# Attention with pooled keys, then a two-layer MLP: second-layer products split into 256-column halves, and other hand-over times in the planner

## The chip, the cores and the metric

The kernel runs on one core of one Trainium2 chip. The metric is the device time of one execution in microseconds; the time given for a kernel is the median of its runs. A core has five engines that run side by side, each through its own list of instructions in order: TensorE (PE in the profile; its weight loads are shown as PEld), ScalarE (ACT), VectorE (DVE), GpSimd (POOL) and SyncE (SP, which here only issues transfers). They wait for one another by semaphores.

## What is computed

```python
# q (4, 12288, 128), kv (4, 384, 32, 128), w_sr (128, 128)
kv_pool = kv.reshape(B, H // 4, 4, W // 4, 4, C).mean(axis=(2, 4))
k = v = kv_pool.reshape(B, -1, C) @ w_sr          # 768 keys per batch
s = (q @ k.transpose(0, 2, 1)) / np.sqrt(C)
a = np.exp(s - s.max(-1, keepdims=True)); a /= a.sum(-1, keepdims=True) + 1e-9
x = (a @ v).reshape(49152, 128)
h = x @ w_in                                      # w_in (128, 2048)
out = (h * (1.0 / (1.0 + np.exp(-1.702 * h)))) @ w_out   # w_out (2048, 128)
```

The arrays are float32; the kernel multiplies in bfloat16 with float32 accumulation.

## The kernel before

**Tiles.** The 49152 rows are cut into 96 groups of `G` = 512. Attention has 6 chunks of 128 keys per group, the MLP 16 chunks (`FCH`) of 128 hidden columns per group. Both run the same two-step pattern. A *fill* is a first-layer product of 512 columns into one bank of PSUM: keys by queries (line 350) or `w_in` by `x` (line 596). ScalarE then applies Exp (line 352) or the gelu (line 598) to `K` = 3 such banks at once, 1536 columns wide, and writes bfloat16 to the large SBUF tile `ag`, which has 34 frames of three chunks. A *drain* reads a chunk back from `ag` as the operand of a second product that accumulates in another bank: `drain_attn` for tiles of 128 queries, three tiles to a bank (line 363, 129 columns, the last being the row sum), and `drain_moe` for one chunk of a group (line 606, 512 columns, weights `w_out_sb[:, fc, :]`). After 16 drains of the MLP, VectorE transposes the bank to `o_sb` (line 617) and SyncE stores it in four transfers. Drains of the very last group have a form of their own, `drain_last`, with products of 128 columns on line 634.

**Banks.** Of the eight banks of PSUM, 0 to 2 and 3 to 5 take the fills alternately, so fill `p` writes the banks that the activation of fill `p - 2` must have read. Banks 6 and 7 (in the start-up, when fills are one or two chunks wide, also 2 and 5) hold the accumulations and the smaller helpers: pooling of the keys, projections, transposes.

**Order.** `R` = 2 rounds: attention of 48 groups, then their MLP, then the same for the other 48. The list `seq` holds the fills with their widths, the list `todo` the drains. Some activations are computed on VectorE instead of ScalarE, by `early_fill` (lines 403 to 477, fills on lines 409 and 415).

**The planner.** Nothing is scheduled by the compiler: the program is recorded in the order that the loop at line 797 chooses, and each engine runs it in that order. The loop keeps a reckoned time `now` on TensorE, in units of one 512-column product. `end[p]` is the reckoned end of activation `p`. After fill `n + 2` it emits drains and helpers until the next would end after

```python
limit = end[-1] - len(seq[n + 3][1]) - HANDOVER
```

that is, so late that the next fill could not be done when the activation before it ends. It then emits the next fill. A drain may begin no sooner than `end[needs] + HANDOVER`; a fill no sooner than `end[p - 2] + HANDOVER / 2`; an activation `HANDOVER / 2` after its fill. With few free frames in `ag` (`room`) the limit is set aside. `free` holds when a bank is reckoned to be empty, `dve` when VectorE is.

Of the kernel before, what the change touches and what calls it, by code (L numbers as in the profile page):

```python
# [24 lines left out]
def kernel(  # L25
    ctx, tc, q, kv, w_sr, moe_w_in, moe_w_out, out,
):
    nc = tc.nc
# [7 lines left out]
    FCH = d_ff // 128  # L36
    scale = 1.0 / (C ** 0.5)
    G = 512
    SG = 4 * G
    NG = B * N // G  # L40
# [3 lines left out]
    K = 3  # L44
    T = 128
    TS = 3
# [38 lines left out]
    def acc(key=None):  # L85

        nonlocal last_acc
        last_acc = next_acc()
        turns.append(last_acc)
        turns.remove(last_acc)  # L90
        if key:
            closes[last_acc] = key
        return banks[:, last_acc, :]
# [7 lines left out]
    def close(key, then):  # L101
        for m in [m for m in closes if closes[m] == key]:
            del closes[m]
            free[m] = then


    now = 0.0
# [165 lines left out]
    for m in range(0, 128, 32):  # L273
        p = slice(m, m + 32)
# [23 lines left out]
    w_out_sb = cpool.tile([128, FCH, C], BF)  # L298
# [28 lines left out]
    def room_ahead():  # L327
        return K * len(free_frames())
# [6 lines left out]
    def weights(c):  # L335
        if c[0] == "a" and c[1] in early:
            return ag[:, (c[1] - early[0]) * JC + c[2], :]
        if c[0] == "a" and c[1:] in rolling:
            return aside[:, rolling.index(c[1:]) % K, :]
        if c[0] == "m" and c[1:] in lent:  # L340
            return aside[:, (len(rolling) + lent.index(c[1:])) % K, :]
        return ag[:, slot_of[c], :]
# [249 lines left out]
    o_of = {}  # L592
# [4 lines left out]
                             x[:, g % (4 * XS) * G:(g % (4 * XS) + 1) * G], start=True, stop=True)  # L597
        nc.scalar.activation(place([("m",) + c for c in chunks]), ps, AF.Gelu_apprx_sigmoid)  # L598

    def drain_moe(g, fc):  # L600
        if g == NG - 1:
            drain_last(g, fc)
            return
        if fc == 0:
            o_of[g] = acc(("o", g))
        nc.tensor.matmul(o_of[g], w_out_sb[:, fc, :], weights(("m", g, fc)),  # L606
                         start=(fc == 0), stop=(fc == FCH - 1))
        if (g, fc) in lent:
            used.append((g, fc))
        else:  # L610
            del slot_of["m", g, fc]
        if fc == FCH - 1:
            close(("o", g), max(now, dve - 1.0) + EVACUATE)
            on_dve(3.6)

            o_sb = opool.tile([128, 512], F32, name="o_sb")
            nc.vector.transpose(o_sb, o_of.pop(g))  # L617
            for m in range(4):
                nc.sync.dma_start(out=out_r[g, m],
                                  in_=o_sb[32 * m:32 * m + 32, :].rearrange("i (b j) -> i b j", j=32))  # L620
# [34 lines left out]
    seq, todo = [], []  # L655
    todo_early = [("a", t, a) for t in range(NT) for a in range(2) if (t // TS * TS + TS - 1) // 4 in early]
    for n in range(R):
        part = [c for c in chunks if c[0] // (NG // R) == n]
        while part:
            m = sizes.pop(0) if sizes else K  # L660
            seq.append(("a", part[:m]))
            part = part[m:]
        begin = n * NT // R
        if n == 0:
            begin = SPLIT * TS
# [7 lines left out]
        while flat:  # L673
            m = K if len(flat) > sum(rest) else rest.pop(0)
# [36 lines left out]
    def prepare(p):  # L711

        nonlocal now
        kind, part = seq[p]
        for i, jc in part:
            if (kind, i) not in begun:
                begun.add((kind, i))
                (background if kind == "a" else background_moe)(i)
            while kind == "a" and ((key_and_value, i // GB, jc) in extras or (transpose_q, i) in extras):
                f, *args = extras.pop(0)  # L720
                now = max(now, free[next_acc()]) + COST[f][0]
                f(*args)
                free[last_acc] = copied(f)
# [19 lines left out]

    FIXED, CHUNK, SWITCH, HANDOVER, EVACUATE = 0.295, 1.978, 6.0, 1.0, 4.5
    COST = {pool_chunk: (1.9, 2.6), key_chunk: (0.3, 2.4), value_chunk: (0.3, 2.4),
            transpose_q: (1.05, 4.2), early_fill: (1.0, 5.5), key_and_value: (0.55, 3.5),
            transpose_pooled: (0.9, 3.6), make_k: (0.8, 3.2), make_v: (0.8, 3.7)}
# [1 line left out]
    SMALL = 0.26  # L751
    RECIPROCAL = 8.2
    PAUSE = 4.0
    end, extra_at = [], 0.0
    source, dve = None, 0.0
    early_left = 2 * (G // T) * EARLY

    def on_dve(cost):
        nonlocal dve
        dve = max(dve, now + 1.0) + cost  # L760
# [8 lines left out]
    def fill(p):  # L769
        nonlocal now  # L770
        if p >= len(seq):
            return
        kind, part = seq[p]
        prepare(p)
        if p == 4:
            turns.insert(0, 2)
        if p == narrow - 5:
            for m in (2, 5):
                turns.remove(m)
        if p == narrow:  # L780
            assert not any(m in closes for m in (2, 5))
            now = max(now, free.pop(2), free.pop(5))
        lo = K * (p % 2)
        (fill_attn if kind == "a" else fill_moe)(part, banks[:, lo:lo + len(part), :])
        if p >= 2:
            now = max(now, end[p - 2] + HANDOVER / 2)
        now += len(part)
        begin = max(now + HANDOVER / 2, end[p - 1] if p else 0.0)
        if p and kind != seq[p - 1][0]:
            begin += SWITCH  # L790
        end.append(begin + FIXED + CHUNK * len(part))
# [4 lines left out]
    jobs(2)  # L796
    for n in range(len(seq)):
        fill(n + 2)
        jobs(n + 3)
        while True:  # L800
            room = room_ahead()
            limit = end[-1] - len(seq[n + 3][1]) - HANDOVER if n + 3 < len(seq) else 1e9
            bank = free[next_acc()]
            f = None
            if extras and now >= max(extra_at, bank):
                f, *args = extras[0]
            if steps and dve <= now + 2.0:
                early_step()
            near = todo and todo[0][0] == "m" and todo[0][2] > 10
            if not f and not near and not steps and early_todo and early_fits(min(n + 2, len(seq) - 1), *early_todo[0]) and dve <= now + 2.0 and now >= bank:  # L810
                f, args = early_fill, early_todo[0]
            if f and max(now, bank) + COST[f][0] > limit + (0.0 if f is early_fill else 4.5) and room >= 4 * K:
                f = None
            if f:
                now = max(now, bank) + COST[f][0]
                f(*args)
                free[last_acc] = dve + 1.0 if f is early_fill else copied(f)
                if f in (transpose_pooled, make_k, make_v):
                    on_dve(2.5)
                extra_at = max(now + PAUSE, dve + 1.5 if f in (transpose_pooled, make_k, make_v) else 0.0)  # L820
                if f is early_fill:
                    pass
                else:
                    extras.pop(0)
                continue
            if not source:

                if todo_early and not any(early_waits(t) for t in range(todo_early[0][1], todo_early[0][1] + TS)):
                    source = todo_early
                else:  # L830
                    source = todo
            if not source:
                break
            kind, i, c = source[0]
            needs = at[("at" if kind == "a" else kind, i, c)]
            cost = K * SMALL if kind == "a" else 1.0
            halved = kind == "a" and i // TS < SPLIT
            first_of = (c == 0 or halved) and (kind == "m" or i % TS == 0)
            if source is not todo_early and (needs > n or (kind == "a" and first_of and at["at", i + TS - 1, c if halved else 1] > n)
                                             or (kind == "m" and first_of and (i, FCH - 1) in lent  # L840
                                                 and made.get((i, FCH - 1), 1e9) > now + 1.0)
                                             or (kind == "a" and (early_waits(i) or first_of and early_waits(i + TS - 1)))):
                if first_of:
                    source = None
                break
            start = now if source is todo_early else max(now, end[needs] + HANDOVER)
            if first_of:
                start = max(start, bank)
            if start + cost > limit and not (room < 2 * K + 1 or (room < 4 * K and start == now)):
                if first_of:  # L850
                    source = None
                break
            now = start + cost
            (drain_attn if kind == "a" else drain_moe)(i, c)
            source.pop(0)
            if kind == "a" and i // 4 in early:
                early_left -= 1
                if not early_left:
                    low = 0
            if (halved or c == (1 if kind == "a" else FCH - 1)) and (kind == "m" or i % TS == TS - 1):  # L860
                source = None
# [31 lines left out]
```

## Time and profile before

| what | value |
|---|---|
| time, median of 3 runs | 948.76 us (948.5 to 948.81) |
| span of the profiled execution | 946.7 us |
| granted TensorE clock | 1.000 |
| ScalarE, gelu on line 598 | 509 instructions, 681.1 us busy, 1489 ns each |
| ScalarE, Exp on line 352 | 192 instructions, 245.6 us busy |
| TensorE, fills on line 596 | 1476 recorded, 379 ns each |
| TensorE, drains on line 606 | 1477 + 17 recorded, 379 ns each |
| weight loads of line 606 | 1520, 98 ns each |
| VectorE, transposes on line 617 | 95 of 717 ns |

A busy time is the union of the records on an engine. A record of a matmul runs from its start to its modelled end, so records of successive matmuls overlap, and so do those of successive activations; what an engine can do per unit of time is read from one start to the next. Some matmul records are missing in a trace, so a gap of one whole product between two records is no idle time; weight loads are counted more fully. The profile has the idle time before an instruction in brackets, with the engine and line whose end ended it.

### The profile page before, as it was taken

What the parts mean: (1) busy time and instruction counts of PE and PEld (TensorE: products, weight loads), DVE (VectorE), ACT (ScalarE), POOL (GpSimd) and SP (SyncE); (2) the same over time, 40 slices, a digit from 0 to 9 for tenths busy, and PEclk for the clock granted to TensorE, in tenths of its full rate; (3) what the DMA queues carried; (4) which work ended last, traced back from release to release, by engine and by line L of the source; (5) the groups of instructions that cost most, each with busy time, mean ns of one, the idle gap of its engine ahead of it and who ended that gap; (6) DMA issues with size and microseconds to landing.
All of it is one profiled execution on the core that took longest, in us unless ns stands there. A gap on an engine that the chain in (4) does not pass through costs nothing.

```text
span 946.7 us, 15374 instructions
## 1 busy us (share of the span) xinstructions
PE 933.9 (99%) x6200; PEld 502.5 (53%) x6314; DVE 575.1 (61%) x1091; ACT 933.5 (99%) x709; POOL 66.5 (7%) x115
## 2 busy tenths in 40 slices
PE   8999999999999999999999999999999999999998
PEld 4677776444444444444446777744444444444444
DVE  5753653011678776667765765376767766777651
ACT  6999999999999999999999999999999999999998
POOL 3101001330000232000000000000000000000000
PEclk9999999999999999999999999999999999999999
DMA  9997943999867799865335683552222222222222
GB/s 210 195 207 168 181 92 52 130 163 170 164 117 114 119 147 119 127 99 87 56 58 105 138 170 84 119 123 42 36 39 40 38 41 34 44 34 45 34 45 46
DMA packets 372856, 95.46 MB, mean 101 GB/s; under 512 B 346720, under 2 KB 370400, under 8 KB 372320
## 3 DMA queue, kind: packets, MB, share of 16 engines
q1 hardware_dynamic: 344000, 62.36, 36.9%
q0 software_dynamic: 28512, 31.99, 22.3%
q8 instruction: 49, 0.80, 0.3%
q14 instruction: 23, 0.19, 0.1%
q10 hardware_dynamic: 272, 0.13, 0.0%
HBM read 52.49 MB, written 48.76 MB: 107 GB/s over the span
## 4 chain that ended last, share of the span: by engine, by line
PE 97%; ACT 1%; DMA 1%; issue 1%; DVE 0%; POOL 0%; POOLq 0%
PE banks L606 35%; PE banks L596 34%; PE banks L363 14%; PE banks L350 12%; ACT ag L352 1%; PE banks L415 1%; DMA x<-in_kv_dram 1%; PE banks L139 0%; PE banks L409 0%; PE banks L634 0%; PE banks L236 0%; POOL x L222 0%; PE banks L161 0%; PE banks L294 0%; PE banks L192 0%
## 5 line engine op out<-in xcount | busy, mean ns | idle before, releaser
L598 ACT ACTIVATE ag<-banks 128x1536 bf16<-128x1536 f32 (+1 forms) x509 | 681.1, 1489 | 0.0
L596 PE MATMUL banks<-x,w_in_sb 128*128 128x512 bf16 x1476 | 405.8, 379 | 1.7
L606 PE MATMUL banks<-ag,w_out_sb 128*128 128x512 bf16 x1477 | 402.6, 379 | 1.7
L352 ACT ACTIVATE ag<-banks 128x1536 bf16<-128x1536 f32 (+2 forms) x192 | 245.6, 1421 | 3.5 <-PE banks L236 2.3
L606 PEld LDWEIGHTS <-w_out_sb 128*128 128x128 bf16 x1520 | 148.3, 98 | 177.2 <-issue 0.2
L596 PEld LDWEIGHTS <-w_in_sb 128*128 128x128 bf16 x1519 | 147.1, 98 | 171.3 <-issue 0.7
L617 DVE STREAM_TRANSPOSE o_sb<-banks 128x512 f32<-128x512 f32 x95 | 68.1, 717 | 171.4 <-PE banks L606 166.9
L363 PEld LDWEIGHTS <-ag 128*128 128x128 bf16 x2268 | 145.5, 98 | 44.6 <-issue 0.3
L363 PE MATMUL banks<-v,ag 128*128 128x129 bf16 x2268 | 163.0, 220 | 0.2
L350 PE MATMUL banks<-qT,kT 128*128 128x512 bf16 x498 | 145.0, 379 | 3.5 <-ACT ag L352 0.5
L442 DVE SCALAR_TENSOR_TENSOR ea<-ea,eb 128x512 f32<-128x512 f32 x132 | 90.4, 685 | 3.7 <-DVE ea L442 0.7
L386 DVE RECIPROCAL rec<-banks 128x3 f32<-128x3 f32 x124 | 22.3, 180 | 85.3 <-PE banks L363 84.9
L389 DVE TENSOR_TENSOR x<-banks,rec 128x384 bf16<-128x384 f32 x124 | 69.1, 557 | 4.3
L350 PEld LDWEIGHTS <-kT 128*128 128x128 bf16 x543 | 45.8, 98 | 25.9 <-issue 2.0
L473 DVE RECIPROCAL eb<-ea 128x256 f32<-128x256 f32 x34 | 57.6, 1724 | 0.5
L466 DVE SCALAR_TENSOR_TENSOR ea<-ea,eb 128x512 f32<-128x512 f32 x68 | 46.5, 683 | 1.9
L173 POOL DMA_DIRECT2D kvs<-in_kv_dram x32 | 40.4, 1323 | 19.3 <-DMA kvs<-in_kv_dram 17.1
L431 DVE TENSOR_SCALAR ea<-banks 128x512 f32<-128x512 f32 x33 | 22.8, 692 | 29.6 <-PE banks L415 29.2
L521 POOL MEMSET gate_tile<- 1x1 f32 x38 | 3.4, 89 | 325.8 <-DVE gate_tile L520 325.8
L453 DVE TENSOR_SCALAR qT<-banks 128x512 f32<-128x512 f32 x17 | 11.8, 692 | 20.7 <-PE banks L409 20.6
L437 DVE SCALAR_TENSOR_TENSOR eb<-eb,ea 128x512 f32<-128x512 f32 x33 | 22.8, 691 | 0.9
L444 DVE SCALAR_TENSOR_TENSOR ag<-ea,ee 128x512 bf16<-128x512 f32 x24 | 16.6, 691 | 1.2
(83 smaller groups left out, 286.3 us busy)
## 6 DMA issues: line engine op xcount, KB each, us to landing
out_dram<-o_sb SPq DMA_DIRECT2D x380, 64.0 KB, 2.0
kvs<-in_kv_dram POOLq DMA_DIRECT2D x32, 384.0 KB, 6.3
q_bf<-in_q_dram POOLq DMA_DIRECT2D x21, 512.0 KB, 6.6
x_bf<-x SPq DMA_DIRECT2D x13, 768.0 KB, 5.6
x<-in_kv_dram POOLq DMA_DIRECT2D x11, 512.0 KB, 10.4
x_bf<-x SPq DMA_DIRECT2D x6, 384.0 KB, 4.6
x<-in_q_dram POOLq DMA_DIRECT2D x5, 256.0 KB, 15.3
x<-in_kv_dram SPq DMA_DIRECT2D x1, 1024.0 KB, 5.0
```

Source lines behind the costliest of these rows:

```text
L173: nc.gpsimd.dma_start(out=kv_sums[b][:, i2], in_=kv_p[b, i, w, :, i2], **({"accum_op": ADD} if n else {}))
L350: nc.tensor.matmul(ps[:, k, :], kTs[i // GB][:, jc * 128:(jc + 1) * 128], rhs, start=True, stop=True)
L352: nc.scalar.activation(place([("a",) + c for c in chunks]), ps, AF.Exp, scale=scale)
L363: nc.tensor.matmul(av_of[u][:, k * (C + 1):(k + 1) * (C + 1)], weights(("a", i, jc))[:, o:o + T], vs[i // GB][:, jc, 0:C + 1], start=(jc = ...
L389: nc.vector.tensor_tensor(to, ps[:, :, 0:C], rec.unsqueeze(2).broadcast_to([128, TS, C]), MUL)
L442: nc.vector.scalar_tensor_tensor(a, a, COEFFS[k], b, ADD, MUL)
L466: nc.vector.scalar_tensor_tensor(a, a, COEFFS[k], b, ADD, MUL)
L473: nc.vector.reciprocal(b[:, m:m + 256], a[:, m:m + 256])
L596: nc.tensor.matmul(ps[:, k, :], w_in_sb[:, fc * 128:(fc + 1) * 128], x[:, g % (4 * XS) * G:(g % (4 * XS) + 1) * G], start=True, stop=True)
L598: nc.scalar.activation(place([("m",) + c for c in chunks]), ps, AF.Gelu_apprx_sigmoid)
L606: nc.tensor.matmul(o_of[g], w_out_sb[:, fc, :], weights(("m", g, fc)), start=(fc == 0), stop=(fc == FCH - 1))
L617: nc.vector.transpose(o_sb, o_of.pop(g))
```

## The change

Three things change. `drain_moe` takes a range of columns, so that a product can be emitted as two of 256 columns, each with its own weight load. The planner's one `HANDOVER` becomes `RELEASE` (from the reckoned end of an activation to whoever waits for it, by kind of activation) and `LATENCY` (from the end of a fill to its activation), and the fixed part of an activation, `FIXED`, goes from 0.295 to 0.25. And where a whole product of the MLP (not a group's first, and not of the last group) would end past `limit` but a half would not, the loop emits the left half, goes on to the next fill, and emits the right half when it gets to the drains again.

```diff
-    def drain_moe(g, fc):
+    def drain_moe(g, fc, lo=0, hi=G):
...
-        nc.tensor.matmul(o_of[g], w_out_sb[:, fc, :], weights(("m", g, fc)),
-                         start=(fc == 0), stop=(fc == FCH - 1))
+        nc.tensor.matmul(o_of[g][:, lo:hi], w_out_sb[:, fc, :], weights(("m", g, fc))[:, lo:hi],
+                         start=(fc == 0), stop=(fc == FCH - 1 and hi == G))
+        if hi < G:
+            return
...
-    FIXED, CHUNK, SWITCH, HANDOVER, EVACUATE = 0.295, 1.978, 6.0, 1.0, 4.5
+    FIXED, CHUNK, SWITCH, EVACUATE = 0.25, 1.978, 6.0, 4.5
+    RELEASE, LATENCY, HALF = {"a": 0.8, "m": 1.6}, 0.95, 0.506
...
-            now = max(now, end[p - 2] + HANDOVER / 2)
+            now = max(now, end[p - 2] + RELEASE[seq[p - 2][0]])
         now += len(part)
-        begin = max(now + HANDOVER / 2, end[p - 1] if p else 0.0)
+        begin = max(now + LATENCY, end[p - 1] if p else 0.0)
...
-            limit = end[-1] - len(seq[n + 3][1]) - HANDOVER if n + 3 < len(seq) else 1e9
+            limit = end[-1] - len(seq[n + 3][1]) - LATENCY if n + 3 < len(seq) else 1e9
...
-            cost = K * SMALL if kind == "a" else 1.0
+            cost = K * SMALL if kind == "a" else HALF if begun_half else 1.0
...
-            start = now if source is todo_early else max(now, end[needs] + HANDOVER)
+            start = now if source is todo_early else max(now, end[needs] + RELEASE[seq[needs][0]])
...
+            if kind == "m" and c and not begun_half and i < NG - 1 and start + cost > limit >= start + HALF:
+                drain_moe(i, c, 0, G // 2)
+                now = start + HALF
+                begun_half = True
+                continue
...
             now = start + cost
-            (drain_attn if kind == "a" else drain_moe)(i, c)
+            if begun_half:
+                drain_moe(i, c, G // 2, G)
+                begun_half = False
+            else:
+                (drain_attn if kind == "a" else drain_moe)(i, c)
```

The built program has 6553 matmuls instead of 6314: 478 of 256 columns take the place of 239 on line 606. All other instructions are the same ones, in another order on TensorE and VectorE.

More of the change, by code (lines that the diff above doesn't have):

```diff
@@ L603, in drain_moe @@
             return
-        if fc == 0:
+        if fc == 0 and lo == 0:
             o_of[g] = acc(("o", g))
-        nc.tensor.matmul(o_of[g], w_out_sb[:, fc, :], weights(("m", g, fc)),
-                         start=(fc == 0), stop=(fc == FCH - 1))
+        nc.tensor.matmul(o_of[g][:, lo:hi], w_out_sb[:, fc, :], weights(("m", g, fc))[:, lo:hi],
+                         start=(fc == 0), stop=(fc == FCH - 1 and hi == G))
+        if hi < G:
+            return
         if (g, fc) in lent:
@@ L754 @@
     end, extra_at = [], 0.0
-    source, dve = None, 0.0
+    source, dve, begun_half = None, 0.0, False
     early_left = 2 * (G // T) * EARLY
@@ L835 @@
             needs = at[("at" if kind == "a" else kind, i, c)]
-            cost = K * SMALL if kind == "a" else 1.0
+            cost = K * SMALL if kind == "a" else HALF if begun_half else 1.0
             halved = kind == "a" and i // TS < SPLIT
-            first_of = (c == 0 or halved) and (kind == "m" or i % TS == 0)
+            first_of = (c == 0 or halved) and (i % TS == 0 if kind == "a" else not begun_half)
             if source is not todo_early and (needs > n or (kind == "a" and first_of and at["at", i + TS - 1, c if halved else 1] > n)
```

## The prediction

> **What bounds the kernel now.** I read the page's first two parts, then the costliest groups, then the timeline at single matmuls, at the start and at the end.
>
> ```profile
> PE 933.9 (99%) x6200; PEld 502.5 (53%) x6314; DVE 575.1 (61%) x1091; ACT 933.5 (99%) x709; POOL 66.5 (7%) x115
> ...
> PE   8999999999999999999999999999999999999998
> ...
> ACT  6999999999999999999999999999999999999998
> ```
>
> TensorE and ScalarE are both at 99%, so occupancy doesn't say which of them sets the time. A TensorE record also holds the matmul's pipeline (379 ns for 512 columns), so I went to the spacing of the starts.
>
> ```profile
> 298.52 14.98 ACT L598 ACTIVATE ag<-banks 128x1536 bf16<-128x1536 f32 x11
> ...
> 301.72 0.81 PE L596 MATMUL banks<-x,w_in_sb 128*128 128x512 bf16 x3
> ...
> 302.37 0.81 PE L606 MATMUL banks<-ag,w_out_sb 128*128 128x512 bf16 x3
> ...
> 303.02 0.81 PE L596 MATMUL banks<-x,w_in_sb 128*128 128x512 bf16 x3
> ```
>
> Each line gives start, length, engine and group. Three matmuls take 0.81 us, so their starts are (0.81 - 0.379) / 2 = 0.215 us apart, and the next three start 0.65 us later, three such steps: no slot is free. Over the whole trace the mean spacing is 215.8 ns behind 512 columns (L596, L606) and 56.7 ns behind 129 (L363). Taking each pair of starts and subtracting the row's spacing (a gap of a whole slot is a missing record), TensorE's gaps come to 0.6 us from 60 us to the end. Before 45 us they come to about 9 us. ScalarE's eleven activations start (14.98 - 1.49) / 10 = 1.349 us apart on average, while the commonest spacing of two 1536-wide ones in the trace is 1.331 us. ScalarE therefore waits a little in nearly every step, and TensorE never does: after 60 us **TensorE's own work sets the time**.
>
> ```profile
> 26.27 0.39 PE L236 MATMUL banks<-ident,x 128*128 128x128 bf16 x4
> 26.97 0.59 PE L350 MATMUL banks<-qT,kT 128*128 128x512 bf16 x2 [0.31 <-ACT ag L352]
> ...
> 940.35 0.59 PE L596 MATMUL banks<-x,w_in_sb 128*128 128x512 bf16 x2
> ...
> 940.78 2.62 PE L634 MATMUL banks<-w_out_sb,ag 128*128 128x128 bf16 x44
> 942.82 0.91 DVE L642 COPY o_sb<-banks 128x128 f32<-128x128 f32 x3 [3.57 <-PE banks L634]
> ```
>
> In the start-up TensorE does wait, for ScalarE here. At the end the last first-layer product starts at 940.35 and only 2.4 us of second-layer work stand behind it: both engines finish together, and copies and stores follow in any order of the work.
>
> **The change part by part.** The built orders of the two kernels have the same activations in the same order, and the same matmuls except that 239 of the 1520 second-layer products on L606 are two of 256 columns.
>
> *The halves, added work.* Two rows give the price of a matmul's beginning: (215.8 - 56.7) / (512 - 129) = 0.4156 ns per column, so 56.7 - 129 x 0.4156 = 3.0 ns remain at zero columns. 239 more beginnings x 3.0 ns = **0.7 us**, on the engine that has no gap. Each half also loads its weights again: 239 x 98 ns = 23.4 us more on PEld, which has 947 - 502 us free. The cover is the matmul that runs meanwhile.
>
> ```profile
> L363 PEld LDWEIGHTS <-ag 128*128 128x128 bf16 x2268 | 145.5, 98 | 44.6 <-issue 0.3
> L363 PE MATMUL banks<-v,ag 128*128 128x129 bf16 x2268 | 163.0, 220 | 0.2
> ```
>
> Here a load of 98 ns stands before each matmul of 129 columns, and they still start 56.7 ns apart with 0.2 us of idle time in 2268: a 256-column half (0.4156 x 256 + 3.0 = 109 ns) covers it better. Without the cover it would be those 23.4 us. The Trainium skill ("TensorE: Matmul & The Clock Gate", section "The mechanism") speaks against the change: weight loads overlap running matmuls only when their row groups differ. All loads here fill 128 rows, so by that rule the sum would be 23.4 us higher; this trace contradicts it, and I take the row.
>
> *The order, moved work.* The new reckoning puts first-layer matmuls (L350, L596) sooner. For each I summed, in both built orders, the durations of all matmuls ahead of it. The difference grows steadily to 8.0 us at the last one: that much second-layer and attention work is left behind it, and where 2.4 us follow the last first-layer product now, about 11 us will. TensorE does not shorten its work by this; it only does the same work later. The price is zero as long as ScalarE can follow, for a first-layer group refills the banks that ScalarE must first have read. So I set "us by which TensorE reaches the group sooner" against "us that ScalarE has waited so far" (starts of two activations less 1.331 us, table loads taken off), both counted from 45 us:
>
> | up to, us | sooner | ScalarE's waits | left |
> |---|---|---|---|
> | 145 | 0.8 | 1.6 | 0.8 |
> | 245 | 1.8 | 2.7 | 0.9 |
> | 345 | 2.3 | 3.5 | 1.2 |
> | 495 | 3.5 | 5.1 | 1.6 |
> | 545 | 4.4 | 5.5 | 1.1 |
> | 645 | 5.2 | 6.7 | 1.5 |
> | 745 | 5.8 | 7.7 | 1.9 |
> | 845 | 6.6 | 8.7 | 2.1 |
> | 920 | 7.4 | 9.4 | 2.0 |
>
> The right column never falls below zero: the advance is nearly the whole of ScalarE's waiting and not more. Both engines are then full at once, and the cover is thin. The deepest fall of the right column at any step is 0.66 us (in the second attention stretch, around 500 to 545 us); where ScalarE cannot be ahead, TensorE waits that long at the bank. Bounds: 0 (fills now are 0.2 us early, which swallows most falls) and 0.66 us; I take **0.3 us**.
>
> *The start-up.* The first moved matmuls come at about 21 us: groups of three L363 matmuls (3 x 56.7 ns = 0.17 us) go from before a first-layer pair to behind it, in about ten places up to 50 us, and at the table's first row the two orders are level again. TensorE's real gaps from 20 to 45 us sum to 1.8 us. If the moves fill all of them the gain is 1.8; if six of ten each open a wait of their own 0.17 us the loss is 1.0. Some moves go one way and some the other, so I take **0**.
>
> *The end.* ScalarE ends some 7 us earlier, TensorE drains alone, and the last product of L634 is again followed by the same copy and store: 946.7 - 942.8 = 3.9 us as now. DVE must empty a bank (L617, 0.72 us) in the time of 16 products, 16 x 215.8 ns = 3.5 us, and two banks alternate, so this hides. Stores (64 KB, four per group, 2.0 us to landing) hide likewise.
>
> *Sum.* On the profiled execution: 946.7 + 0.7 + 0.3 + 0 = 947.7. The median of the runs, 948.76, is 2.1 us above that span, and this does not change: **949.8 us**.
>
> **The rivals.**
>
> *ScalarE sets the time, so its waits are worth their length (faster).* The Trainium skill ("Perfetto Trace Analysis", section "Identifying the Most-Contended Engine") judges TensorE's headroom by MFU and by the weight loads' busy share, and ScalarE's by occupancy. By the 53% of PEld against ScalarE's 99%, ScalarE would be the bound, and the advance of 8.0 us would be gained: 941.5 by that reading. Against it stands the spacing in this trace: 0.6 us of gaps in 880 us. What TensorE can still gain lies before 45 us: 948.76 - 1.8 + 0.7 = 947.7, which is not yet faster by 0.2%. Chance of more: 4%.
>
> *ScalarE cannot give up its waits (slower).* Place: the hand-over from the last first-layer matmul to ScalarE, in every step. Its quickest in the trace is 0.415 us from that matmul's start to the activation's, which the new plan uses almost in full (0.95 of a 0.2158 us slot, plus the slot itself: 0.421 us). Activations that start 1.348 us apart, 17 ns late, are common now even where their matmuls ended in time. If that lateness stays, the advance of up to 7.4 us turns into TensorE's waiting: at most 948.76 + 0.7 + 7.4 = 956.9; if a third stays, 948.76 + 0.7 + 2.5 = 952.0. It decides once more than the spare 2.0 us of the table's last row (its right column) is kept: from there on each microsecond kept is one lost. For it: the margin is thin. Against it: a late ScalarE gets its matmuls earlier, and there the lateness is rarer (with 0.54 to 0.62 us from matmul to activation nearly all spacings are 1.331 us). 26%, mostly near its lower end.
>
> *The halves' loads are not covered (slower).* 948.76 + 23.4 + 0.7 = 972.9. The L363 rows exclude it for equal tiles; 1%, counted in the 26%.
>
> *The change does nothing that can be measured.* That is the forecast itself, with the work merely put off: 70%.
>
> **How the numbers follow.** A measurement of this kernel can tell about 0.2% from no change, which is 1.9 us: 946.9 to 950.7. The likeliest case has 949.8, and its bounds are 948.76 - 1.8 + 0.7 = 947.7 and 948.76 + 0.7 + 0.66 + 1.0 = 951.1, of which the last 0.4 us already lie past 950.7; I count that among the slower ones. The range reaches from 947.7 to the third-kept case, 952.0. Faster 0.04, same 0.70, slower 0.26.
>
> **What would show it.** Right: the record counts on L606 rise by about 239; TensorE's starts after 60 us keep their spacing, with the gaps' sum under 1.5 us; the commonest spacing of activations is 1.331 us and the last 1024-wide one starts near 934 instead of 941 us; between it and the first copy on L642 (old numbering) lies a run of second-layer matmuls alone. Wrong: waits of first-layer matmuls (L350, L596) for ScalarE in the steady stretches, by more than a microsecond in all, or a total below 946.9 us, which would mean that TensorE's slots were not the bound.

## The result and the profile after

The changed kernel takes 956.56 us (median of 4 runs, 956.53 to 956.6), the kernel before 948.78 us in the same comparison: slower by 7.8 us, ratio 1.0083 with an interval of 1.0069 to 1.0097. The forecast was 949.8 us with a range from 947.7 to 952.0, so it was wrong. The profiled execution has a span of 954.8 us.

The page's parts on the engines, the 40 slices and the chain that ended last, of the changed kernel:

```profile
PE 946.4 (99%) x6553; PEld 525.9 (55%) x6553; DVE 572.3 (60%) x1091; ACT 932.4 (98%) x709; POOL 66.7 (7%) x115
...
PE   8999999999999999999999999999999999999998
...
ACT  6999999999999999999999999999999999999994
...
PE 84%; ACT 13%; DMA 1%; DVE 0%; issue 0%; SPq 0%; POOL 0%; DVEq 0%; POOLq 0%
```

Busy shares hardly differ from before. Two things do: ScalarE's last slice is 4 instead of 8, so it stops earlier than TensorE now, and 13% of the chain that ended last has moved from TensorE to ScalarE (1% before). The halves are where they were announced: 474 of them in the row below and 4 in a smaller row, each 272 ns long, 107 ns shorter than a whole product for 256 columns less (groups by shape of the changed kernel; the columns behind the first bar are busy us and mean ns of one, the last is idle time):

```profile
L606 PE MATMUL banks<-ag,w_out_sb 128*128 128x512 bf16 x1266 | 354.4, 379 | 0.0
...
L606 PE MATMUL banks<-ag,w_out_sb 128*128 128x256 bf16 x474 | 129.2, 272 | 0.0
```

The steady stretch of the changed kernel in the timeline (start, length, engine, group):

```profile
703.13 0.81 PE L606 MATMUL banks<-ag,w_out_sb 128*128 128x512 bf16 x3
703.77 0.81 PE L596 MATMUL banks<-x,w_in_sb 128*128 128x512 bf16 x3
704.42 0.81 PE L606 MATMUL banks<-ag,w_out_sb 128*128 128x512 bf16 x3
705.09 0.81 PE L596 MATMUL banks<-x,w_in_sb 128*128 128x512 bf16 x3
705.74 0.38 PE L409 MATMUL banks<-x,w_in_sb 128*128 128x512 bf16 x1
```

Three products take 0.65 us from start to start. The last step but one takes 0.67: TensorE stood still for 24 ns before the fill at 705.09, and that fill started 51 ns after the end of the activation whose banks it refills. After 60 us, 191 fills of lines 350 and 596 have such a gap of over 8 ns, most of 15 to 55 ns, 7.3 us in all (no matmul is missing from this trace), and 190 of them start 50 to 52 ns after the end of an activation. The view of waits shows the longer ones, under the engine of the weight loads; before, and then after (us in all, times, longest):

```profile
PEld L596 <- issue: 0.7, 3, 0.2
```

```profile
PEld L596 <- issue: 7.7, 45, 0.3
```

From its first to its last matmul, TensorE's time less the sum of all its matmuls (at 0.4156 ns per column and 3.05 ns each) is 11.1 us before and 18.0 us after: 6.9 us more standing still. The 239 additional matmuls make 0.7 us more, and the end after the start of the last matmul 0.4 us (946.68 - 943.18 = 3.50 before, 954.75 - 950.82 = 3.93 after). That is the 8.1 us between the two spans, but for rounding.

The end, in the timeline of the changed kernel:

```profile
939.93 7.07 PE L606 MATMUL banks<-ag,w_out_sb 128*128 128x512 bf16 x32
...
946.84 0.67 PE L636 MATMUL banks<-w_out_sb,ag 128*128 128x128 bf16 x9
947.04 0.72 DVE L619 STREAM_TRANSPOSE o_sb<-banks 128x512 f32<-128x512 f32 x1 [2.74 <-DMA out_dram<-o_sb]
947.81 3.23 PE L636 MATMUL banks<-w_out_sb,ag 128*128 128x128 bf16 x55 [0.31 <-DVE o_sb L619]
```

Some 11 us of second-layer work lie behind the last fill, as the built order says, against 2.5 us before. ScalarE's last activations, before and then after:

```profile
934.50 7.57 ACT L598 ACTIVATE ag<-banks 128x1024 bf16<-128x1024 f32 x8
```

```profile
937.82 2.92 ACT L598 ACTIVATE ag<-banks 128x1024 bf16<-128x1024 f32 x3
```

The last of them starts at 939.6 us now, and not near 934: it was 941.0 before. TensorE put 8 us of work off, and ScalarE came only 1.4 us sooner for it.

### The profile page after: what moved, and what is told of

It is laid out like the page before. It is cut to its first block, busy times and chain, and to the rows that moved or that the text cites. A ratio compares the mean times of both kernels' runs of the same rounds, so it can differ in the third digit from the quotient of the medians.

```text
span 954.8 us, 15982 instructions
## 1 busy us (share of the span) xinstructions
PE 946.4 (99%) x6553; PEld 525.9 (55%) x6553; DVE 572.3 (60%) x1091; ACT 932.4 (98%) x709; POOL 66.7 (7%) x115
## 4 chain that ended last, share of the span: by engine, by line
PE 84%; ACT 13%; DMA 1%; DVE 0%; issue 0%; SPq 0%; POOL 0%; DVEq 0%; POOLq 0%
PE banks L596 35%; PE banks L606 33%; ACT ag L352 13%; PE banks L363 8%; PE banks L350 6%; DMA x<-in_kv_dram 1%; PE banks L415 1%; PE banks L409 0%; DMA out_dram<-o_sb 0%; PE banks L636 0%; DVE o_sb L619 0%; PE banks L139 0%; SPq L621 0%; POOL x L222 0%; DVE kT L163 0%
## 5 line engine op out<-in xcount | busy, mean ns | idle before, releaser
L596 PE MATMUL banks<-x,w_in_sb 128*128 128x512 bf16 x1519 | 410.4, 378 | 0.0
L606 PE MATMUL banks<-ag,w_out_sb 128*128 128x512 bf16 (+1 forms) x1740 | 408.2, 350 | 0.0
L606 PEld LDWEIGHTS <-w_out_sb 128*128 128x128 bf16 x1759 | 171.4, 98 | 180.9 <-issue 1.0
L350 PE MATMUL banks<-qT,kT 128*128 128x512 bf16 x543 | 148.4, 378 | 1.8 <-DVE kT L163 0.4
```

Source lines behind the costliest of these rows:

```text
L350: nc.tensor.matmul(ps[:, k, :], kTs[i // GB][:, jc * 128:(jc + 1) * 128], rhs, start=True, stop=True)
L596: nc.tensor.matmul(ps[:, k, :], w_in_sb[:, fc * 128:(fc + 1) * 128], x[:, g % (4 * XS) * G:(g % (4 * XS) + 1) * G], start=True, stop=True)
L606: nc.tensor.matmul(o_of[g][:, lo:hi], w_out_sb[:, fc, :], weights(("m", g, fc))[:, lo:hi], start=(fc == 0), stop=(fc == FCH - 1 and hi == G))
```

## What ScalarE's records say

The prediction took the commonest distance of two starts, 1.331 us, for ScalarE's own pace. Successive 1536-wide activations near 702 us, read from the records one by one (start in ns, length, to the next start, to the next end):

```text
before: 701904 1470 1331 1343      after: 701974 1727 1354 1342
        703235 1482 1331 1344             703328 1715 1347 1344
        704566 1495 1387 1344             704675 1712 1331 1342
        705953 1452 1347 1342             706006 1723 1336 1345
        707300 1447 1331 1344             707342 1732 1347 1342
```

The starts jump; the **ends** are 1.342 to 1.345 us apart, in both kernels. The same instruction is 1.45 to 1.74 us long in these records, and longer in the kernel whose fills come earlier, as the groups by shape show, before and after:

```profile
L598 ACT ACTIVATE ag<-banks 128x1536 bf16<-128x1536 f32 x501 | 673.6, 1496 | 0.0
```

```profile
L598 ACT ACTIVATE ag<-banks 128x1536 bf16<-128x1536 f32 x501 | 673.2, 1697 | 0.0
```

Same busy time, 0.2 us longer records: they start earlier and end no sooner. That an engine's pace is read from one start to the next, as the table of the profile before was explained, therefore doesn't hold for ScalarE here. By the ends, ScalarE's waits in the 654 wide steps after 45 us come to 1.0 us before (mean distance 1.3449 us, against 1.3433 in the changed kernel) and to nothing after. Counted as the prediction did, by the starts less 1.331 us, the same steps give 9.1 us.

The Trainium skill ("Perfetto Trace Analysis", section "DVE / Act Engine Instruction (TENSOR_ADD, Activation, etc)") puts the reported start where the instruction begins to execute and the reported end where its writes are acknowledged. The end agrees with these runs in so far as a waiting fill starts 50 to 52 ns behind it. A start that moves by 0.25 us while the ends keep their pace doesn't fit a start of execution.

So theory A was formed: `FIXED` + 3 x `CHUNK` is the planner's idea of an activation. With 0.295 it is 6.229 slots x 215.8 ns = 1.3442 us, just above the measured 1.3433 to 1.3435; with 0.25 it is 6.184 slots = 1.3345 us, 9 ns below it. In some 690 steps the plan runs 6.2 us ahead of what ScalarE can do, and TensorE stands at the banks.

## The experiments

The times of the first four are beside 948.49 us of the kernel before, those of the last three beside 948.38 us.

**One constant back,** in the changed kernel:

```diff
-    FIXED, CHUNK, SWITCH, EVACUATE = 0.25, 1.978, 6.0, 4.5
+    FIXED, CHUNK, SWITCH, EVACUATE = 0.295, 1.978, 6.0, 4.5
```

> The changed kernel with FIXED back at 0.295, all else as changed (224 products halved). Theory A (FIXED = 0.25 reckons an activation at 6.184 slots of 215.8 ns = 1.3345 us, while in both traces the ends of two activations lie 1.3435 us apart; 9 ns short in each of some 690 steps sends TensorE 6 to 8 us ahead, and it waits for ScalarE): with 0.295 the plan has 1.3442 us, the fills are no longer drawn ahead (0.4 us at the last, against 7.8), TensorE's gaps after 60 us fall from 6.6 to under 1.5 us, and the time is before plus the halves, 948.8 + 0.7 = 949.5, at most 951. Theory B (RELEASE and LATENCY, the narrower window, make the waits): as slow as the change, 955 to 957. Theory C (the halves cost more than 3 ns each): 955 to 957 too, with normal spacing before first-layer matmuls but longer ones at the halves.

Measured: 949.81 us, ratio 1.0013 (1.0004 to 1.0023). Theory A holds: TensorE's gaps at fills fall from 7.3 to 0.5 us, with the halves and the new hand-over times in place. Waits, and the wide activations, of this kernel:

```profile
PEld L596 <- issue: 1.0, 6, 0.2
```

```profile
L598 ACT ACTIVATE ag<-banks 128x1536 bf16<-128x1536 f32 x501 | 673.7, 1494 | 0.0
```

The records are short again: ScalarE is no longer handed its work early.

**The constant alone,** in the kernel before:

```diff
-    FIXED, CHUNK, SWITCH, HANDOVER, EVACUATE = 0.295, 1.978, 6.0, 1.0, 4.5
+    FIXED, CHUNK, SWITCH, HANDOVER, EVACUATE = 0.25, 1.978, 6.0, 1.0, 4.5
```

> The kernel before with FIXED = 0.25 alone: no halves, one HANDOVER. In its built order the last fill is drawn 8.0 us ahead, as in the changed kernel (7.8). Theory A: TensorE waits at fills for some 6 to 7 us, 955 to 957 us, last activation no more than 2 us sooner than before. Theories B and C: 948.8, as before.

Measured: 955.79 us, ratio 1.0076 (1.0061 to 1.0091). Without a half and without a new hand-over time it loses nearly all that the change loses. Its waits:

```profile
PEld L596 <- issue: 9.9, 56, 0.4
```

**The halves alone:** the changed kernel, with its `drain_moe` and the new branch of the loop, but with every constant and every use of `HANDOVER` as before (against the changed kernel; the other two uses are left out here):

```diff
-    FIXED, CHUNK, SWITCH, EVACUATE = 0.25, 1.978, 6.0, 4.5
-    RELEASE, LATENCY, HALF = {"a": 0.8, "m": 1.6}, 0.95, 0.506
+    FIXED, CHUNK, SWITCH, HANDOVER, EVACUATE = 0.295, 1.978, 6.0, 1.0, 4.5
+    HALF = 0.506
...
-            limit = end[-1] - len(seq[n + 3][1]) - LATENCY if n + 3 < len(seq) else 1e9
+            limit = end[-1] - len(seq[n + 3][1]) - HANDOVER if n + 3 < len(seq) else 1e9
...
-            start = now if source is todo_early else max(now, end[needs] + RELEASE[seq[needs][0]])
+            start = now if source is todo_early else max(now, end[needs] + HANDOVER)
```

> The kernel before with the halves alone (238 products halved, FIXED 0.295, HANDOVER as before). Theory A: 948.8 + 238 x 3.0 ns = 949.5, within 0.5. Theory B: the same. Theory C: 955 to 957.

Measured: 949.30 us, ratio 1.0008 (0.9999 to 1.0018). The 238 halved products cost about 0.8 us (between nothing and 1.7 us by the interval), which fits the 3 ns each that were reckoned, and bring nothing. The rule of the Trainium skill that the prediction weighed, that weight loads overlap running matmuls only when their row groups differ ("TensorE: Matmul & The Clock Gate", section "The mechanism"), would have made them cost 238 x 98 ns = 23 us; the measurement decides against it here.

**ScalarE by itself.** In the kernel before:

```diff
-        nc.tensor.matmul(o_of[g], w_out_sb[:, fc, :], weights(("m", g, fc)),
-                         start=(fc == 0), stop=(fc == FCH - 1))
+        if fc not in (3, 7, 11):
+            nc.tensor.matmul(o_of[g], w_out_sb[:, fc, :], weights(("m", g, fc)),
+                             start=(fc == 0), stop=(fc == FCH - 1))
```

> The kernel before with the second-layer products of chunks 3, 7 and 11 left out of each sum (of all groups but the last): 61.5 us less work on TensorE, ScalarE's work unchanged. It measures ScalarE by itself. Theory A (ScalarE was full already; its floor is 1.3435 us from end to end, and the 1.331 us between starts is only how early it is handed its next instruction): ends stay 1.343 us apart, records of activations are long (about 1.7 us), and the time is no more than 2 us below before: 946.5 to 949. Rival (the floor is 1.331 us, and the 9.4 us above it were waits for TensorE): ends 1.331 us apart and 938 to 941 us.

Measured: 948.09 us, ratio 0.9996 (0.9986 to 1.0005). With 61.5 us less to do, TensorE gives back 0.4 us, too little to tell from nothing. Its waits and the wide activations:

```profile
PEld L596 <- issue: 113.2, 444, 0.6
```

```profile
L598 ACT ACTIVATE ag<-banks 128x1536 bf16<-128x1536 f32 x501 | 673.2, 1698 | 0.0
```

TensorE now waits in nearly every step of the MLP, the fill again 51 ns after the activation's end, and ScalarE's ends stay 1.343 us apart (185 of 186 distances from 200 to 450 us are 1.342 to 1.344). This is the pace that nothing but ScalarE sets. The rival's 938 to 941 us falls, and with it the prediction's figure of 1.331 us.

**The change without its halves:**

```diff
-            if kind == "m" and c and not begun_half and i < NG - 1 and start + cost > limit >= start + HALF:
+            if False and kind == "m" and c and not begun_half and i < NG - 1 and start + cost > limit >= start + HALF:
```

> The changed kernel without its halves (FIXED 0.25, RELEASE and LATENCY as changed, every second-layer product whole). The window in which a fill may be emitted is 6.184 - 1.6 - 3 - 0.95 = 0.63 slots, less than one product, so the planner often leaves the rest of a step empty and puts the products off: the last fill is drawn 16.2 us ahead in the built order. Theory A (what the plan draws ahead comes back as TensorE's waiting, less about 1.5 us): 962 to 965 us; the halves then repair a loss that the narrow window itself makes. Rival (the new window is harmless and FIXED alone costs): 955 to 956, as with FIXED = 0.25 alone.

Measured: 968.05 us, ratio 1.0207 (1.019 to 1.0224), worse than both theories had it, and well beyond the rival. The timeline of this kernel shows the empty piece of each step:

```profile
704.09 0.81 PE L596 MATMUL banks<-x,w_in_sb 128*128 128x512 bf16 x3
704.74 0.81 PE L606 MATMUL banks<-ag,w_out_sb 128*128 128x512 bf16 x3
705.44 0.81 PE L596 MATMUL banks<-x,w_in_sb 128*128 128x512 bf16 x3
706.08 0.81 PE L606 MATMUL banks<-ag,w_out_sb 128*128 128x512 bf16 x3
```

From fill to fill 1.35 us, one activation, with 6 slots = 1.295 us of work: 50 ns are lost in every such step, since a seventh product doesn't fit into the window. In its waits:

```profile
PEld L596 <- issue: 60.7, 358, 0.2
```

The halves do what they are for: with the narrow window, leaving them out costs 11.9 us more (19.7 against 7.8 above the kernel before). But the window of the kernel before was wide enough for whole products (6.229 - 0.5 - 3 - 1.0 = 1.73 slots, against 6.184 - 1.6 - 3 - 0.95 = 0.63 here), and halves gained nothing there.

**More and less of the constant,** in the changed kernel, 0.27 and 0.32 in place of 0.25.

> The changed kernel with FIXED = 0.27: an activation reckoned at 6.204 slots = 1.3388 us, 4.7 ns short of the measured 1.3435; last fill drawn 4.9 us ahead in the built order, 175 products halved. If the loss follows the shortfall: between 949.8 (0.295) and 956.6 (0.25), at 952.5 to 953.8 us. If it has a threshold instead: at one of the two ends.

Measured: 953.27 us, ratio 1.0051 (1.0036 to 1.0066). The loss follows the shortfall: 4.9 us at 0.27 lies between the 1.3 us at 0.295 and the 7.8 us at 0.25, and no threshold shows between them. The waits lie between as well:

```profile
PEld L596 <- issue: 3.7, 18, 0.4
```

> The changed kernel with FIXED = 0.32: an activation reckoned at 6.254 slots = 1.3496 us, 6 ns longer than measured; in the built order fills come up to 2.3 us later than before (0.9 at the last), so ScalarE waits instead. Expected: TensorE's gaps under 1.5 us, ends of activations 1.346 to 1.349 us apart, last activation 1 to 2 us later than before, and the time 949.5 to 951.5 us. If only a plan that is too fast costs anything: 949.5, as with 0.295.

Measured: 952.38 us, ratio 1.0041 (1.0026 to 1.0056), more than expected. The plan errs to the other side by 6 ns in each step, 690 x 6 ns = 4.2 us, which fits the loss of 4.0 us. I had read it off the built order alone, where the fills are at most 2.3 us late; but an activation that is reckoned too long also lets fills come late by the clock, and the last activation starts at 945.0 us, 3.9 later than before. The wide activations of this kernel are the shortest of all, 1463 ns, and have idle time before them:

```profile
L598 ACT ACTIVATE ag<-banks 128x1536 bf16<-128x1536 f32 x501 | 676.4, 1463 | 0.7 <-PE banks L596 0.4
```

**The account.** Three numbers of each kernel explain its time: the halved products x 3.05 ns; how far the built order draws the last fill ahead of where it was before; and the change of ScalarE's waits by the ends (1.04 us before). The first two are known from the built order; the third is read from each kernel's own trace, so the table is an account and no forecast. All in us:

| kernel | halves | drawn ahead | ScalarE's waits | sum | measured |
|---|---|---|---|---|---|
| the change | 0.73 | 7.84 | -1.05 | 7.5 | 7.8 |
| `FIXED` 0.295 | 0.68 | 0.44 | -0.26 | 0.9 | 1.3 |
| before, `FIXED` 0.25 | 0 | 8.03 | -1.05 | 7.0 | 7.3 |
| halves alone | 0.73 | -0.28 | +0.05 | 0.5 | 0.8 |
| without halves | 0 | 16.23 | +2.02 | 18.3 | 19.7 |
| `FIXED` 0.27 | 0.53 | 4.91 | -0.74 | 4.7 | 4.9 |
| `FIXED` 0.32 | 0.68 | -0.91 | +4.17 | 3.9 | 4.0 |

What is drawn ahead of a full ScalarE is not done sooner; it is left over at the end. The kernel with three products in 16 left out fits in as well: the same work stands behind its last fill as before, ScalarE's waits fall by 0.4 us, and it measured 0.4 us less. The sums of the table stay 0.1 to 0.5 us short (1.4 without halves); the last transposes and stores, which lie closer together behind a longer drain (0.31 us of waiting for VectorE and 0.4 us after the last matmul in the changed kernel), are part of that, and the rest was not looked into.

No version that does the whole work ran faster than the kernel before. With TensorE relieved of 61.5 us the time stays at 948.1 us, so there was little to gain by the order: after 45 us no more than the 1.0 us that ScalarE waits.

## Why the prediction was wrong

- **What bounds the kernel** was half right. TensorE has no gap after 60 us, as shown. But "ScalarE therefore waits a little in nearly every step" was read off the starts and is false: by the ends it waited 1.0 us in 654 steps. Both engines were full.
- **The step that failed is "The order, moved work".** Its table set the advance of up to 7.4 us against ScalarE's waits of 9.4 us, counted as starts less 1.331 us, and found the advance covered, at 0.3 us (bound 0.66). With the true pace the waits were 1.0 us, so some 6.8 us of the 7.8 by which the built order is ahead (8.0 by the prediction's sum) had no cover. TensorE stood still for 6.9 us more than before.
- **The halves** were sized right: 239 x 3.0 ns = 0.7 us forecast, 0.8 us measured for 238 of them alone, and their weight loads stayed hidden.
- **The start-up**, taken as 0, did not show: up to 50 us the gaps sum to 10.8 us before and 9.3 us after, and about 1.9 us of the former are records missing from the trace (78 matmuls of line 350 beside 87 weight loads), which leaves 8.9 against 9.3.
- **The end**, taken as no change, cost 0.4 us after the last matmul and a wait of 0.31 us for VectorE.
- **The slower rival** said that ScalarE cannot give up its waits, and as its limit 956.9 us; 956.6 came. It got 26% and was thought to stay near its lower end, because lateness seemed rarer where fills came early. That impression, too, came from the starts: an activation that is handed over early shows an early start. But its reason, a lateness of 17 ns in the hand-over from fill to ScalarE, was read off the starts as well and is not what the runs show: with fills early everywhere, the ends still lie 1.343 us apart. There were hardly any waits to give up, and that its limit came so close is in part luck.
- **What was to show it wrong** did: fills wait for ScalarE in the steady stretches by far more than a microsecond (7.3 us), and the last activation came at 939.6 us instead of near 934. One sign of being right came all the same and meant nothing: the commonest distance of two starts is still 1.331 us in the changed kernel (277 of 654).

## What to carry to other kernels

Take an engine's pace from the distance of its ends in a stretch where it surely never waits, or relieve the other engine and measure it: ScalarE's recorded starts moved here with the arrival of its operands, while its ends kept their pace. In a plan that balances two full engines, a cost that is wrong by half a per cent or so in either direction comes back in full: 9 ns too little in each of 690 steps cost 7.3 us here, 6 ns too much some 4 us; a constant that looks too large may be the one that is right. Before covering a move of work with another engine's waiting time, show that the waiting is there.

## Not expected of the hardware

- Records of one and the same 1536-wide activation last 1.46 us on average where fills come late (`FIXED` 0.32) and 1.70 us where they come early (the changed kernel), with 1.343 us as the commonest distance of their ends in both.
- A fill that waits for an activation starts 50 to 52 ns after the end of its record, in every kernel run here where such waits are frequent. From the start of a fill's last matmul to its activation's start it takes 0.415 us or more, and 0.415 to 0.416 us is the commonest when fills come late (`FIXED` 0.32).
